# A table of moves goes out of a scheduled attention-and-MLP kernel, thresholds by segment come in, and TensorE is counted as finishing in order

## The chip, the cores and the metric

One core of one Trainium2 chip. The core has five engines with queues of their own: TensorE (PE, its weight loads shown apart as PEld), VectorE (DVE), ScalarE (ACT), GpSimd (POOL) and SyncE (SP), which issues the transfers. The metric is the device time of one launch in microseconds (us); the time before is a median of 802.64 us over three runs (802.03 to 802.87).

## What is computed

A transformer block with modulation by a condition vector, in bf16, for one sequence of 2048 rows, width 640, 32 heads of 20 columns, and an inner MLP width of 1536:

```python
mod = (silu(c) @ w_mod).reshape(1, 6, 1, 640)     # sa, ca, ga, sb, cb, gb
h = layernorm(x) * (1 + ca) + sa
q, k, v = split(h @ wqkv)                         # 32 heads of 20
o = softmax(q @ k.T * 20 ** -0.5) @ v             # 2048 x 2048 scores for each head
x = x + ga * (o @ wo)
h = layernorm(x) * (1 + cb) + sb
x = x + gb * (((h @ w_gate) * (h @ w_up)) @ w_down)
```

The scores alone are 32 x 2048 x 2048 elements, and each needs an exponential.

## The kernel before

**A scheduler in Python writes the program.** The kernel's code first makes tasks: a task is a small group of instructions of one engine with its dependencies, a modelled duration and a priority. `Sched.run` then plays the engines through in modelled time, and whatever an engine picks in that play is appended to its order (`sc.order`). `emit_program` walks over all tasks in the order of their modelled starts, gives each the semaphore waits it still needs, and writes each engine's queue. On the chip each queue runs strictly in that order; nothing is decided there.

**The work.** The 2048 query columns are cut into a chunk of 512 and six of 256. For each chunk and each of eight sets of four heads there is an item. Its work comes in units of 512 columns. A *score* group (line 2126 of the kernel before, `QT,KT`) writes units into PSUM banks. Two units at a time go to ACT, which takes the exponential of 1024 columns and writes them into a ring of 16 slots in `PP` (line 3095). The rest, about two ninths of all units, goes to DVE and POOL in quads of four units: DVE evacuates each unit as 16-bit integers into `DB` (2153), splits the quad into mantissa and exponent (2189, 2197), and a product of the mantissa part (2194 on DVE in one instruction of 2048 columns, or 2209 on POOL in four pieces of 512) gives `DSS`. A *value* group (2806, `PP,Vf` or `DSS,Vf`) multiplies both kinds with V and sums them in PSUM. At an item's end the sums are transposed and divided (2280 to 2323) into `Ocp`.

**What lies beside it.** All other TensorE work is called X by the scheduler: transposes of normalized rows (1693, 2450, 2428), projections for Q, K and V (1732, 1796, and 1536 with `wV`), modulation (1557, and 1536 with `wmb`), the output projection (`wo,Ocp`), gate and up (`h2T,stg`), and down (`wd,hprod`), the last three once for every chunk after its attention. Names ending in t belong to the next-to-last chunk, names ending in c to the last one (`h2Tc`, `hprodc`, `xckc`), whose MLP stands at the end of the program. Lines 1536 and 1532 are helpers that issue groups in 32-column tiles and in full tiles. Matmuls of `ident,Vf` (3259) add zeros and serve only to keep TensorE busy.

**How PE picks.** `pick_pe` runs whenever PE is free in the play: a score group if a pair of banks is free, else X work, value groups or filling, by thresholds that are module globals: how long PE may be held for the next score (`HOLD`), how full the exponentials' ring must be before X goes first (`XFIRST`, `XCONT`), how many value units make a group (`PVMIN`, `PVMAX`, `PVCAP`, `PVTOL`), how far an X group may delay a score (`X_LATE`, `X_HALF`), priorities of DVE's parts (`TPRIO`, `XDPRIO`) and so on. The table `STAGE` gives them values of their own for each item; `stage(it)` sets them.

**The table of moves.** After the play, `replan` edits the result: it drops 18 PE tasks, gives each task that starts after 80 us of modelled time a PSUM bank from a string of digits (`rebank`), takes tasks out of an engine's list and puts them in at other places, computes what then depends on what by bank (`rechain`), and plays the new lists through once more in their given order. The table `PLAN` holds 2034 such moves for PE, 320 for DVE, 245 for SP, 24 for POOL and 1 for ACT.

**Waits.** In `emit_program`, `kn` holds for each engine how far it knows each semaphore to have come. A wait on a task also brings what that task's engine knew when it was issued. PE has several semaphores of its own: `s_pes` for scores, `s_pep` for value groups, `s_pex` for X. What PE itself had finished on the others was not part of what it knew.

Of the kernel before, what the change touches and what calls it, by code (L numbers as in the profile page):

```python
# [37 lines left out]
T0 = 700.0  # L38
# [6 lines left out]
STEAL_END = 66197.894  # L45
# [445 lines left out]
def rebank(sc):  # L491

    k = 0
    for r in sc.G.recs:
        r["move"] = r["task"] is not None and r["task"].start >= PLAN_FROM
        if r["move"]:
            r["i"] = int(PLAN["banks"][k])
            r["put"](r["i"])
            k += 1
    assert k == len(PLAN["banks"])  # L500


def rechain(sc):

    pos = {id(t): i for i, t in enumerate(sc.order["pe"])}
    rows = {}
    for r in sc.G.recs:
        if r["task"] is None and r["i"] in (2, 5):
            continue
        rows.setdefault(r["i"], []).append((pos[id(r["task"])] if r["task"] is not None else -1, r))  # L510
    for lst in rows.values():
        lst.sort(key=lambda x: x[0])
        was = []
        for p, r in lst:
            if r["move"]:
                t = r["task"]
                old = {id(x) for x in r["rel"]}
                keep = {id(x) for x in r["base"]}
                t.deps = [x for x in t.deps if id(x) not in old or id(x) in keep]
                have = {id(x) for x in t.deps}  # L520
                t.deps = t.deps + [x for x in was if id(x) not in have]
            was = list(r["by"])


def replan(sc):
    gone = set(PLAN.get("drop", ()))
    sc.order["pe"] = [t for i, t in enumerate(sc.order["pe"]) if i not in gone]
    rebank(sc)
    for eng, moves in PLAN.items():
        if eng in ("drop", "banks"):  # L530
            continue
        old = sc.order[eng]
        gone = {a for a, _ in moves}
        new = [t for i, t in enumerate(old) if i not in gone]
        for a, b in moves:
            new.insert(b, old[a])
        sc.order[eng] = new
    rechain(sc)
    kept = {id(t) for lst in sc.order.values() for t in lst}
    span = {id(t): t.done - t.start for t in sc.all if id(t) in kept}  # L540
    left = sum(len(x) for x in sc.order.values())
    for t in sc.all:
        t.done = None
# [2823 lines left out]
```

## Time and profile before

| | |
|---|---|
| median of three runs | 802.64 us (802.03 to 802.87) |
| span of the profiled execution, first to last instruction | 800.7 us |
| DMA | 61.91 MB, mean 77 GB/s |
| exponentials on ACT (L3095) | 798 |
| evacuations of DVE's share (L2153) | 452 |
| products of a quad on DVE (L2194) | 39 |
| pieces of products on POOL (L2209) | 296 |
| matmuls | 16556 |

The profile is of one execution; the three times come from executions without it, and no time of the profiled one is given beside its span. Rows of a view by stretch read: start and end, length, then for each engine busy us and number of instructions, granted clock, share of DMA and GB/s. Rows of a timeline read: start, duration, engine, line, operation, tiles, count, and in brackets the idle time before it and who ended it. Rows of the chain read: start, duration, what. In groups by line the columns are busy us and mean ns of one, then idle time before them by releaser. A busy share of PE says that some matmul was in flight, not that PE ran at its peak.

### The profile page before, as it was taken

The page shows a single profiled execution, that of the slowest core. Times are in us where ns is not written, and L with a number is a line of the kernel's source. Part 1 is how long each engine was busy: PE and PEld are TensorE (multiplying, and loading weights), DVE is VectorE, ACT ScalarE, POOL GpSimd, SP SyncE. Part 2 cuts the span into 40 slices and gives each one's busy share as a digit, 9 for nine tenths or more (in the row PEclk, how much of TensorE's full clock was granted, in tenths as well). Part 3 has the DMA queues.
Part 4 walks back from the last instruction along what each step waited for, and adds up shares of the span by engine and source line. Part 5 has one row for each costly group of instructions (what it writes and reads, how often), then busy time and mean ns, then how long its engine had stood idle before and what let it go on. Part 6 is the DMA issues. An engine that isn't in the chain of part 4 may idle for free.

```text
span 800.7 us, 36941 instructions
## 1 busy us (share of the span) xinstructions
PE 787.5 (98%) x16556; PEld 379.1 (47%) x16556; DVE 715.3 (89%) x1308; ACT 750.8 (94%) x835; POOL 423.0 (53%) x416
## 2 busy tenths in 40 slices
PE   8999999999999999999999999999999999999998
PEld 4433523332244344444555545554556555445677
DVE  7979878888999899999989889998999999999964
ACT  6899899999999999999999999999998999999921
POOL 2327575767665655655365565545536447525610
PEclk9999999999999999999999999999999999999999
DMA  9553112112131542010223214241152224124820
GB/s 300 154 144 106 50 51 66 53 52 68 39 88 43 157 107 59 23 30 3 70 58 77 63 28 116 59 104 24 31 126 53 53 60 110 28 61 112 190 48 27
DMA packets 146093, 61.91 MB, mean 77 GB/s; under 512 B 113215, under 2 KB 145935, under 8 KB 145935
## 3 DMA queue, kind: packets, MB, share of 16 engines
q1 hardware_dynamic: 145007, 58.40, 28.7%
q8 instruction: 130, 2.13, 1.1%
q10 hardware_dynamic: 928, 1.15, 0.4%
q14 instruction: 28, 0.23, 0.1%
HBM read 50.53 MB, written 8.99 MB: 74 GB/s over the span
## 4 chain that ended last, share of the span: by engine, by line
PE 66%; ACT 22%; DVE 5%; issue 4%; DMA 1%; POOL 1%; SPq 0%; DVEq 0%; ACTq 0%
PE ps_all L2126 23%; ACT PP L3095 22%; PE ps_all L1536 20%; PE ps_all L2806 14%; PE ps_all L1796 4%; PE ps_all L1532 3%; DVE DB L2153 1%; DVE DSS L2189 1%; DVE DSS L2197 1%; POOL DSS L2209 1%; PE ps_all L1732 1%; PE ps_all L1693 1%; DMA q_rows<-KPA 1%; PE ps_all L2450 0%; DMA x<-in_A_x_dram 0%
## 5 line engine op out<-in xcount | busy, mean ns | idle before, releaser
L3095 ACT ACTIVATE PP<-ps_all 128x1024 bf16<-128x1024 f32 x798 | 734.1, 1163 | 9.7 <-PE ps_all L2806 5.0
L2209 POOL TENSOR_TENSOR DSS<-DB,DSS 128x512 bf16<-128x512 bf16 x296 | 350.3, 1208 | 273.2 <-DVE DSS L2197 229.6
L2126 PE MATMUL ps_all<-QT,KT 32*128 32x256 bf16 (+2 forms) x3648 | 322.9, 286 | 6.6 <-ACT PP L3095 1.9
L2153 DVE TENSOR_SCALAR DB<-ps_all 128x512 int16<-128x512 f32 x452 | 296.4, 680 | 34.0 <-PE ps_all L2126 32.0
L2126 PEld LDWEIGHTS ps_all<-QT,KT 32*128 32x128 bf16 x3648 | 98.0, 92 | 214.0 <-ACT PP L3095 143.0
L2806 PE MATMUL ps_all<-PP,Vf 128*32 128x256 bf16 (+3 forms) x2844 | 162.4, 288 | 0.0
L1536 PE MATMUL ps_all<-h2T,stg 128*32 128x256 bf16 (+2 forms) x2812 | 117.5, 278 | 0.2 <-DVE DB L2153 0.2
L2806 PE MATMUL ps_all<-DSS,Vf 128*32 128x256 bf16 (+3 forms) x1608 | 101.1, 288 | 0.4 <-POOL DSS L2209 0.3
L2806 PEld LDWEIGHTS ps_all<-PP,Vf 128*32 128x32 bf16 (+1 forms) x2844 | 68.1, 95 | 44.1 <-issue 37.2
L2189 DVE TENSOR_SCALAR DSS<-DB 128x2048 int16<-128x2048 int16 x113 | 86.1, 762 | 2.6
L2197 DVE TENSOR_SCALAR DSS<-DB 128x2048 int16<-128x2048 int16 x113 | 80.8, 715 | 0.2 <-PE ps_all L2806 0.2
L1536 PEld LDWEIGHTS ps_all<-h2T,stg 128*32 128x32 bf16 x2812 | 56.3, 95 | 42.5 <-issue 35.0
L1536 PE MATMUL ps_all<-wd,hprod 128*32 128x320 bf16 (+1 forms) x1396 | 59.2, 279 | 0.0
L2806 PEld LDWEIGHTS ps_all<-DSS,Vf 128*32 128x32 bf16 (+1 forms) x1608 | 44.8, 96 | 17.5 <-issue 13.5
L2194 DVE TENSOR_TENSOR DSS<-DB,DSS 128x2048 bf16<-128x2048 bf16 x39 | 48.0, 1230 | 0.4
L2291 POOL TENSOR_TENSOR OTn<-OT,invT 128x160 bf16<-128x160 f32 (+1 forms) x44 | 27.8, 650 | 19.5 <-DVE invT L2286 19.5
L1536 PEld LDWEIGHTS ps_all<-wd,hprod 128*32 128x32 bf16 x1396 | 27.1, 95 | 23.0 <-issue 17.1
L1536 PE MATMUL ps_all<-wV,hT 128*32 128x160 bf16 x1280 | 35.3, 234 | 0.0
L1796 PE MATMUL ps_all<-hT,wk 128*32 128x512 bf16 (+1 forms) x360 | 31.5, 384 | 0.0
L1796 PE MATMUL ps_all<-hT,wq 128*32 128x512 bf16 x375 | 29.8, 384 | 0.0
L1536 PEld LDWEIGHTS ps_all<-wV,hT 128*32 128x32 bf16 x1280 | 23.3, 96 | 13.6 <-issue 8.6
L1536 PE MATMUL ps_all<-wo,Ocp 128*32 128x320 bf16 (+1 forms) x660 | 29.0, 282 | 0.1
(126 smaller groups left out, 513.3 us busy)
## 6 DMA issues: line engine op xcount, KB each, us to landing
stg<-in_B_w_gate_dram SPq DMA_DIRECT2D x74, 160.0 KB
stg<-in_B_w_up_dram SPq DMA_DIRECT2D x74, 160.0 KB
KT<-k_rows SPq DMA_DIRECT2D x28, 128.0 KB
QT<-q_rows SPq DMA_DIRECT2D x48, 64.0 KB
wm<-in_w_mod_dram SPq DMA_DIRECT2D x3, 800.0 KB
x<-in_A_x_dram SPq DMA_DIRECT2D x7, 320.0 KB
k_rows<-KPA SPq DMA_DIRECT2D x16, 128.0 KB
wd<-in_B_w_down_dram SPq DMA_DIRECT2D x1, 1920.0 KB
```

What stands on the lines that cost most here:

```text
L1532: return lambda e, b: e.matmul(ps[:, b, c0:c0 + n], lhs(), rhs(), start=st, stop=sp)
L1536: return lambda e, b: e.matmul(ps[32 * x:32 * x + 32, b, c0 + o:c0 + o + w], lhs()[:, 32 * x:32 * x + 32], rhs() if w == n else rhs()[:, o ...
L1796: f = [lambda e, b_, k=k, x=x: e.matmul(ps[x:x + min(32, w - x), b_, :], wx[:, k, r0 + x:r0 + min(x + 32, w)], hT[tc][:, k, :], tile_posit ...
L2126: ems.append(lambda e, i=i, kt=kt: e.matmul(dstf()[:, i * u.n:(i + 1) * u.n], KT[32 * u.s:32 * u.s + 32, u.j, kt * 128:(kt + 1) * 128], QT ...
L2153: return e.tensor_scalar(DBl[st_["slot"]][:, x * 512:(x + 1) * 512], bank(cell["b"]), EBIAS, 0.0, op0=ALU.add, op1=ALU.max)
L2189: return e.tensor_scalar(DSl[st_["ss"][0]][:, :], DBl[st_["slot"]][:, :], 0x7F, 0x3F00, op0=ALU.bitwise_and, op1=ALU.bitwise_or)
L2194: return e.tensor_tensor(d, DBl[st_["slot"]][:, :].bitcast(BF16), d, ALU.mult)
L2197: return e.tensor_scalar(DSl[st_["ss"][1]][:, :], DBl[st_["slot"]][:, :], 0x7F80, 2, op0=ALU.bitwise_and, op1=ALU.bitwise_or)
L2209: return e.tensor_tensor(d, DBl[st_["slot"]][:, x * w:x * w + w].bitcast(BF16), d, ALU.mult)
L2291: return lambda e: e.tensor_tensor(OTn[:, g0:g0 + gn, DH * (j + x):DH * (j + x) + DH, :].rearrange("p b c r -> p b r c"), OT[:, nq_ * x:nq ...
L2806: ems.append(lambda e, i=i, kt=kt, stt=stt, stp=stp: e.matmul(ps[32 * s:32 * s + mc, binfo["bank"], c0:c0 + u.n], Vf[:, (kt * H + 4 * u.j ...
L3095: return e.activation(o, ps[:, b0:b0 + nu, :], AFT.Exp, scale=ESCALE)
```

## The change

Three parts. `PLAN`, `rebank`, `rechain` and `replan` are taken out, so that the order of the play is the order of the program. A second table of thresholds, `SEGT`, is laid over `STAGE`: `segment()` counts the exponentials that have been scheduled and sets the thresholds anew after every eight, for 76 of the hundred segments; a new threshold `XG` moves the gates of X work. And `emit_program` counts a PE task as known to PE once it is issued, on whatever semaphore: a wait for a later matmul then covers every earlier one.

```diff
-def replan(sc):
-    gone = set(PLAN.get("drop", ()))
-    sc.order["pe"] = [t for i, t in enumerate(sc.order["pe"]) if i not in gone]
-    rebank(sc)
...
             t.know[t.ctr] = t.val
+            if eng == "pe":
+                kn[t.ctr] = t.val
...
-PLAN_FROM = 80000.0
-PLAN = {
-    "drop": (1947, 1963, 2320, 2729, 3517, 3524, 4144, 4160, 4513, 4556, 4634, 4752, 4753, 5229, 5296, 5408, 5573, 5574),
...
+SEG = 8
+SEGT = {
+    1: {"PVTOL": 152.9, "XFIRST": 5},
+    2: {"HOLD": 0, "PVCAP": 10, "PVTOL": 152.9, "TPRIO": 0.538, "XFIRST": 5},
...
+    78: {"EAGER": 9, "PV_KEEP": 1},
+    79: {"PVCAP": 16, "XFIRST": 6, "X_HALF": 61.9},
...
     def stage(it):
         globals().update(base)
         globals().update(STAGE.get(it, {}))
+        globals().update(SEGT.get(seg[0], {}))
+
+    def segment():
+        while sc.progress >= SEG * (seg[0] + 1):
+            seg[0] += 1
+            stage(st_pv["item"])
...
-                    if task.gate > sc.progress or (warm and task.name[:3] == "col" and t > STEAL_END):
+                    if task.gate > sc.progress + XG or (warm and task.name[:3] == "col" and t > STEAL_END):
...
                 sc.progress = max(sc.progress, ap // 2)
+                segment()
...
     join_reads(sc)
-    replan(sc)
     nw = emit_program(nc, sc)
```

The file gets 304 lines shorter, so a line number after the tables is 312 lower in the new program up to line 2498 (2126 becomes 1814, 2806 becomes 2494, 1536 becomes 1224) and 304 lower behind that (3095 becomes 2791; 303 for the filling ones, 3259 becomes 2956).

**What it moves.** The counts of scores, exponentials on ACT, evacuations and value groups stay. Products of 2048 columns on DVE go from 39 to 53, pieces on POOL from 296 to 240. Gate and up of the middle chunks are cut more finely (matmuls of 256 columns 1880 to 1772, of 128 columns 576 to 728, of 512 columns 356 to 372), down less finely (320 columns 908 to 972, 160 columns 488 to 360). Filling goes from 40 matmuls of 512 columns to 16 of 512 and 88 of 256. ACT gets one evacuation of `hT` and one of `gsb` more. Second waits of exponentials, on `s_pep`, go from 500 to 3.

PE near the 632nd exponential, where the scores are those of the last but one chunk (`QT_78`) and the X work belongs to chunks ahead of it; before:

```order
L1536 MATMUL ps_all<-wo_109,Ocp_92 32x320 x24
L2126 MATMUL ps_all<-QT_78,KT_70 128x256 x10
L1536 MATMUL ps_all<-h2T_106,stg_110 32x256 x20
L1536 MATMUL ps_all<-h2T_106,stg_108 32x256 x20
L1536 MATMUL ps_all<-h2T_106,stg_114 32x256 x20
L1536 MATMUL ps_all<-h2T_106,stg_111 32x256 x20
L1536 MATMUL ps_all<-h2T_106,stg_114 32x256 x20
L1536 MATMUL ps_all<-h2T_106,stg_111 32x256 x8
L2126 MATMUL ps_all<-QT_78,KT_70 128x256 x10
```

and now:

```order
L1814 MATMUL ps_all<-QT_78,KT_70 128x256 x4
L2494 MATMUL ps_all<-DSS_88,Vf_83 32x256 x6
L2494 MATMUL ps_all<-DSS_88,Vf_83 21x256 x2
L1224 MATMUL ps_all<-wd_103,hprod_105 32x320 x8
L2494 MATMUL ps_all<-PP_84,Vf_83 32x256 x20
L1814 MATMUL ps_all<-QT_78,KT_70 128x256 x8
L1224 MATMUL ps_all<-wd_103,hprod_105 32x320 x28
L1224 MATMUL ps_all<-wd_103,hprod_105 32x160 x4
L1814 MATMUL ps_all<-QT_78,KT_70 128x256 x4
L2494 MATMUL ps_all<-PP_84,Vf_83 32x256 x8
```

Before, 108 gate and up matmuls stood between two score groups; now no more than 36 matmuls do, value groups included, and PE is at a down product there where it was at gate and up.

PE at the end, from the last score group (`QT_79` is the last chunk's queries) to the last block's gate and up (`h2Tc`); before:

```order
L2126 MATMUL ps_all<-QT_79,KT_70 128x128 x16
L1536 MATMUL ps_all<-h2Tt_120,stg_111 32x256 x4
L1536 MATMUL ps_all<-h2Tt_120,stg_114 32x256 x16
L2806 MATMUL ps_all<-PP_84,Vf_83 32x128 x16
L1532 MATMUL ps_all<-wo_109,Ocp_92 128x320 x12
L1536 MATMUL ps_all<-h2Tt_120,stg_114 32x256 x4
...
L2806 MATMUL ps_all<-PP_84,Vf_83 32x128 x20
L1532 MATMUL ps_all<-wo_109,Ocp_92 128x320 x6
L2428 MATMUL ps_all<-ident_49,xn2c_131 128x128 x5
L1536 MATMUL ps_all<-wd_103,hprodt_119 32x320 x100
L1532 MATMUL ps_all<-wo_109,Ocp_92 128x320 x2
```

(three groups of 20 `h2Tt` matmuls are left out, and behind the last row come 92 more `hprodt` ones), and now:

```order
L2494 MATMUL ps_all<-PP_84,Vf_83 32x128 x28
L1814 MATMUL ps_all<-QT_79,KT_70 128x128 x8
L1224 MATMUL ps_all<-wd_103,hprodt_119 32x160 x4
L1224 MATMUL ps_all<-wd_103,hprodt_119 32x320 x20
L2494 MATMUL ps_all<-PP_84,Vf_83 32x128 x28
L1220 MATMUL ps_all<-wo_109,Ocp_92 128x320 x18
L1224 MATMUL ps_all<-wd_103,hprodt_119 32x320 x16
L2494 MATMUL ps_all<-PP_84,Vf_83 32x128 x8
L1224 MATMUL ps_all<-wd_103,hprodt_119 32x320 x28
L2116 MATMUL ps_all<-ident_49,xn2c_131 128x128 x5
L1224 MATMUL ps_all<-wd_103,hprodt_119 32x320 x4
L1220 MATMUL ps_all<-wo_109,Ocp_92 128x320 x2
```

(then 64 `hprodt` and the `h2Tc` matmuls). All gate and up of the next-to-last chunk now stand ahead of the last score, and so do 48 full and 20 half down matmuls; the last score is a group of 8, not of 16.

PE near the 62nd exponential, where modulation (`wmb,SCb`) and the V projection run beside the first items; before, a part of it:

```order
L2126 MATMUL ps_all<-QT_73,KT_70 128x512 x3
L1536 MATMUL ps_all<-wmb_33_81,SCb_117 32x320 x12
L1536 MATMUL ps_all<-wmb_33_81,SCb_117 32x160 x8
L1536 MATMUL ps_all<-wmb_33_81,SCb_117 32x320 x12
L2126 MATMUL ps_all<-QT_73,KT_70 128x512 x4
L1536 MATMUL ps_all<-wmb_33_81,SCb_117 32x320 x12
L1536 MATMUL ps_all<-wV_102,hT_100 32x160 x20
L1536 MATMUL ps_all<-wmb_34_82,SCb_117 32x320 x20
L2126 MATMUL ps_all<-QT_73,KT_70 128x512 x5
L2806 MATMUL ps_all<-PP_84,Vf_83 32x512 x3
L1536 MATMUL ps_all<-wmb_34_82,SCb_117 32x320 x20
L1536 MATMUL ps_all<-wV_102,hT_100 32x160 x36
```

and now:

```order
L1814 MATMUL ps_all<-QT_73,KT_70 128x512 x2
L2956 MATMUL ps_all<-ident_49,Vf_83 32x512 x4
L1224 MATMUL ps_all<-wV_102,hT_100 32x160 x20
L1224 MATMUL ps_all<-wmb_34_82,SCb_117 32x320 x40
L2494 MATMUL ps_all<-DSS_90,Vf_83 32x512 x3
L2494 MATMUL ps_all<-DSS_90,Vf_83 21x512
L2494 MATMUL ps_all<-PP_84,Vf_83 32x512 x9
L2494 MATMUL ps_all<-DSS_89,Vf_83 32x512 x4
L2494 MATMUL ps_all<-DSS_88,Vf_83 32x512 x4
L1224 MATMUL ps_all<-wV_102,hT_100 32x160 x28
L1814 MATMUL ps_all<-QT_73,KT_70 128x512 x3
L2494 MATMUL ps_all<-PP_84,Vf_83 32x512 x8
```

Pieces of 32 to 56 X matmuls between scores have become one piece of 60, with filling ahead of it and all waiting value groups behind it.

More of the change, by code (lines that the diff above doesn't have):

```diff
@@ L488, in join_reads @@
                 r[k] = mapped(r[k])
[L491 to L522, printed above, removed]
@@ L1170 @@
+XG = 0
+SEGK = ("XG", "XFIRST", "XCONT", "PV_OPEN", "FILL_HARD")
 XHALF = 1
@@ L2940, in pick_x @@
             for task in rl:
-                if task.gate > sc.progress or (warm and task.name[:3] == "col" and t > STEAL_END):
+                if task.gate > sc.progress + XG or (warm and task.name[:3] == "col" and t > STEAL_END):
                     continue
```

132 lines of the change are left out of this document (75 added, 57 removed), and 296 rows, old and new, of the table PLAN.

## The prediction, made before the run

> **What bounds the kernel now.** I read the page's busy shares first, then the busy time by stretch, then the groups by line, the waits, and last ACT's and PE's timelines. The page:
>
> ```profile
> PE 787.5 (98%) x16556; PEld 379.1 (47%) x16556; DVE 715.3 (89%) x1308; ACT 750.8 (94%) x835; POOL 423.0 (53%) x416
> ```
>
> PE looks like the bound. It isn't for most of the span. The stretches (span's start to end; PE, PEld, DVE, ACT, POOL busy us):
>
> ```profile
> 50.00:100.00 50.00, 49.51 (x944) 20.72 (x936) 43.73 (x82) 47.11 (x52) 30.78 (x26) 1.00 0.35 96
> 100.00:600.00 500.00, 495.63 (x10219) 220.80 (x10215) 456.90 (x789) 498.66 (x544) 290.93 (x271) 1.00 0.25 64
> 600.00:625.00 25.00, 25.00 (x618) 14.44 (x611) 23.93 (x47) 21.93 (x25) 15.44 (x18) 1.00 0.41 87
> 625.00:750.00 125.00, 123.28 (x2979) 63.43 (x2978) 118.79 (x196) 125.00 (x137) 65.81 (x61) 1.00 0.32 71
> 750.00:766.20 16.20, 15.38 (x464) 10.70 (x455) 12.76 (x25) 13.94 (x15) 6.09 (x5) 1.00 0.85 189
> 766.20:800.70 34.50, 31.83 (x600) 27.37 (x597) 19.71 (x55) 3.04 (x8) 1.10 (x2) 1.00 0.07 24
> ```
>
> From 100 to 600 us ACT is busy 498.66 of 500 us and from 625 to 750 all of it; TensorE's granted clock is 1.00 throughout. What ACT does there, and who waits for it:
>
> ```profile
> L3095 ACT ACTIVATE PP<-ps_all 128x1024 bf16<-128x1024 f32 x798 | 734.1, 1163 | 9.7 <-PE ps_all L2806 5.0 <-PE ps_all L2126 4.7
> PEld ps_all L2126 <- ACT PP L3095: 143.0, 489, 0.6
> ```
>
> 798 exponentials cost 734.1 us, 0.920 each in series (their 1163 ns overlap). PE's weight loads for scores wait for ACT 489 times, 143.0 us in all: in the steady part PE's time is partly slack, in small pieces. So the span is: a head before the first exponential, the exponentials with ACT's holes, and a tail of PE work behind the last one. Only holes and tail can move, as the count of exponentials on ACT is 798 in both orders.
>
> Four places lose time. ACT's timeline at the end:
>
> ```profile
> 759.09 3.77 ACT L3095 ACTIVATE PP<-ps_all 128x1024 bf16<-128x1024 f32 x4 [0.86 <-PE ps_all L2126]
> 764.19 1.94 ACT L3095 ACTIVATE PP<-ps_all 128x1024 bf16<-128x1024 f32 x2 [1.33 <-PE ps_all L2126]
> 780.70 0.81 ACT L2436 ACTIVATE h2Tc<-ps_all,mcol 128x128 bf16<-128x128 bf16 x2 [14.57 <-PE ps_all L2428]
> ```
>
> The last exponential ends at 764.19 + 1.94 = 766.13; idle times of 0.86 + 1.33 = 2.19 us stand shortly ahead of it (hole 3). Between 766.13 and 800.7 lie 34.6 us of tail. Hole 2, at 606 us (PE, then ACT):
>
> ```profile
> 606.34 3.13 PE L1536 MATMUL ps_all<-h2T,stg 128*32 128x256 bf16 x108
> 610.90 1.94 ACT L3095 ACTIVATE PP<-ps_all 128x1024 bf16<-128x1024 f32 x2 [2.68 <-PE ps_all L2806]
> ```
>
> PE runs 108 gate/up matmuls in one piece, 3.13 us, with no score between them; ACT has two exponentials in store (1.94 us), then idles 2.68 us. With small ones ACT loses 25 - 21.93 = 3.07 us in that window. Hole 1 lies between 50 and 100 us: 50 - 47.11 = 2.89 us.
>
> **The change part by part.** Terms are against the profiled execution: span 800.7; the median 802.64 is 1.9 us above it, taken as launch and end, the same for both.
>
> (a) *Tail.* PE's part of the chain there:
>
> ```profile
> 763.82 0.35 PE ps_all L2126 x16
> 764.18 0.66 PE ps_all L1536 x20
> 765.10 1.84 PE ps_all L1532 x12
> 766.94 1.86 PE ps_all L1536 x64
> 768.80 0.47 PE ps_all L2806 x20
> 770.19 0.28 PE ps_all L2428 x5
> 770.47 3.51 PE ps_all L1536 x100
> 774.47 3.24 PE ps_all L1536 x92
> 779.60 1.00 PE ps_all L1532 x18
> 780.66 17.38 PE ps_all L1532 x252
> ```
>
> Behind the last score (763.82) PE still does 20 + 64 = 84 gate/up matmuls of the tail block, 0.66 + 1.86 = 2.52 us, and 192 down matmuls (100 + 92), 6.75 us, or 35.2 ns each. In the new order all 84 are ahead of the last score, and of the down matmuls 132 full ones and 4 of half width are left: 134 x 35.2 ns = 4.72 us. So 2.52 + 6.75 - 4.72 = **4.6 us less** PE work behind the last score. The rest there is the same in number: 36 value matmuls, 20 of the output projection, 240 gate/up and 60 down ones of the last 128-column block.
>
> That work was cover, so I ask what is late next. In DVE's timeline the last big transpose of value sums, then residual and evacuation of the first of the last two row tiles; in PE's the last projection matmuls, for the second tile:
>
> ```profile
> 762.37 0.45 DVE L2280 STREAM_TRANSPOSE OT<-ps_all 128x256 f32<-128x256 f32 x1
> 766.16 0.49 DVE L2391 TENSOR_TENSOR xckc<-ps_all,xckc 128x320 bf16<-128x320 f32 x1 [1.02 <-PE ps_all L1532]
> 770.40 1.35 DVE L2440 TENSOR_SCALAR h2Tc<-ps_all,mcol 128x128 bf16<-128x128 bf16 x5
> 773.91 0.45 PE L1532 MATMUL ps_all<-wo,Ocp 128*128 128x320 bf16 x2
> ```
>
> The first tile's chain, from 766.16 to 771.75, takes 5.6 us. In the new order PE has beside it 8 of 18 projection matmuls (1.84/12 = 0.153 us each: 1.2), 8 value matmuls (0.2), 112 down matmuls (3.9), and two projection and five transposing ones (0.6): 5.9 us. That just covers. The projection itself now stands directly behind a group of value matmuls, with 56 value, 24 down and 8 score matmuls (1.3 + 0.8 + 0.2 = 2.3 us by these rows) between the value sums it needs and itself, where before it started 765.10 - 762.37 = 2.7 us behind their transpose. I put 1.5 us of new PE idle time, between 0 and 4.6 (all of the gain given back). The second tile's chain, from the last projection matmuls to its last evacuation, is covered by 64 down matmuls and 120 gate/up ones: 2.3 + 120 x 1.00/18 = 8.9 us, against the 7.6 from 773.91 to 781.51 (ACT's row of h2Tc above). **Tail: -3.1**, ends -4.6 and 0. The work pulled ahead of the last score lies beside ACT, in the 143.0 us of slack.
>
> (b) *Hole 2.* The run of 108 is gone; near that point no more than 36 matmuls now stand between two scores, 36 x 35.2 ns = 1.3 us, under the 1.94 that ACT holds in store. **-3.0**, ends -3.07 and 0.
>
> (c) *Hole 1.* Here the new order has one clump ahead of a value wait: 4 filling matmuls, 20 V and 40 modulation ones, 4 + 9 for value sums. With the rows below (3.4/40, 3.6/84, 35.3/1280 us each; value matmuls of 512 columns like the filling ones) it is 0.34 + 0.55 + 1.71 + 1.1 = 3.7 us, less 1.94 in store: 1.8 us of ACT idle in place of 2.89. **-1.0**, ends -2.89 and +2.
>
> ```profile
> L3259 PE MATMUL ps_all<-ident,Vf 128*32 128x512 bf16 x40 | 3.4, 384 | 0.0
> L1536 PE MATMUL ps_all<-wmb,SCb 128*32 128x320 bf16 (+1 forms) x84 | 3.6, 294 | 0.1
> L1536 PE MATMUL ps_all<-wV,hT 128*32 128x160 bf16 x1280 | 35.3, 234 | 0.0
> L2194 DVE TENSOR_TENSOR DSS<-DB,DSS 128x2048 bf16<-128x2048 bf16 x39 | 48.0, 1230 | 0.4
> L1699 ACT ACTIVATE hT<-ps_all,mcol 128x512 bf16<-128x512 bf16 x5 | 3.8, 778 | 4.8 <-PE ps_all L1693 4.8
> ```
>
> (d) *Hole 3.* The last scores now stand every 8 matmuls, with 0.3 to 1.1 us of other work between. I take **-1.5**; ends -2.19 (closed) and +4.6, if all that (a) pulls ahead lands in front of these scores.
>
> (e) *ACT.* One more hT evacuation, 778 ns: **+0.7**, ends 0 (ACT idle there) and +0.8. A gsb cast more, behind the last exponential: 0.
>
> (f) *DVE and POOL.* 14 more products of 2048 columns on DVE, 14 x 1.230 = 17.2 us, in place of 56 pieces on POOL. DVE's rows above leave it 43.1 us between 100 and 600 and 6.2 between 625 and 750, 49.3 in all. Where it was fullest (118.79 of 125) ACT still ran 125.00. I take **0**; ends 0 and +17.2.
>
> (g) *Filling and narrower pieces.* Fill goes from 40 x 512 columns to 16 x 512 and 88 x 256: 40 to 60 full ones, 20 x 3.4/40 = 1.7 us more PE time, in PE's gaps beside ACT: **0**, ends 0 and +1.7. The split forms carry as many columns as before.
>
> (h) *Waits.* 500 of 798 exponentials had a second wait, on the value matmuls that had read their buffer; 3 keep one. The value matmuls stand ahead of the score on PE, so the score's own wait ends later. The row of L3095 shows 5.0 us of idle time by that releaser, of it 2.68 in hole 2, already counted. **0**, ends -2.3 and 0.
>
> POOL's pieces show what the two engines do to each other:
>
> ```profile
> L2209 POOL TENSOR_TENSOR DSS<-DB,DSS x296: 1145/1157/2199, 50.3 to 760.0; 128x512 bf16<-128x512 bf16 x148
> ```
>
> The median piece, 1157, is nearly the fastest, so they seldom disturb each other. [...]
>
> Sum: -3.1 - 3.0 - 1.0 - 1.5 + 0.7 = -7.9; 802.64 - 7.9 = **794.8**.
>
> **The rivals.**
> *All holes close and the tail is covered*: -4.6 - 3.07 - 2.89 - 2.19 = -12.8, 789.9. For it: each hole has one run of PE work as its cause. Against: the clump in (c).
> *The tail turns from PE work to its chains*: (a) gives nothing and (d) nothing: 802.64 - 3.0 - 1.0 + 0.7 = 799.3. For it: 5.9 us of cover over a chain of 5.6.
> *DVE sets the pace, and the kernel is slower*: it evacuates the scores of its own share, and PE's banks stay held until it has. It decides once more than 6.2 us of new products fall into a stretch as full as 625 to 750. With half of the 17.2 on the path, and the four gains lost as scores come late, 802.64 + 8.6 = 811; with the gains kept it would be 803.3. Against: 49.3 us free, and POOL waits for DVE, not DVE for POOL.
> *New holes elsewhere*: the whole order is made anew, so waits that the scheduler does not foresee fall in new places. Two or three more like hole 2 (3.07 each): 800.9 to 804.0.
> *The thresholds change nothing*: excluded, PE's order has 2885 rows in place of 2772.
>
> **How the numbers follow.** Forecast (792 to 798) 0.40; chains in the tail 0.18; all closed 0.14; new holes 0.15 (of it 0.05 still faster); DVE 0.13 (0.01 of it no change). A difference of 0.2% (1.6 us) is about what a measurement of this kernel tells from none. Faster: 0.40 + 0.18 + 0.14 + 0.05 = 0.77; same 0.11; slower 0.12. The range runs from 790 to 803: below it half of "all closed" (0.07), above it nearly all of DVE's case (0.12).
>
> **What would show it.** Right: the new page's ACT idle before L2791 (the exponential's new line) well under 9.7; no run of gate/up matmuls over 2 us near 606; last exponential near 761 and some 31 to 32 us from there to the end. Wrong in (a): idle PE in the tail ahead of the projection or of the last block's gate/up matmuls. Wrong in (f): DVE over 98% in several stretches while ACT loses time there with scores as releaser. Wrong altogether: ACT's holes as large, in other places.

## The result and the profile after

798.22 us, the median of four executions (797.22 to 799.35), beside 802.43 for the kernel before on the same chip: a ratio of 0.9945, 95% interval 0.9931 to 0.9959. Run again twelve times beside the first experiments it took 797.74 us, ratio 0.9955 (0.9939 to 0.9971). The kernel is faster by 4.2 to 4.5 us; 7.8 were forecast, and the range (790 to 803) holds the time.

The page of the kernel after, busy time by engine:

```profile
PE 785.2 (98%) x16628; PEld 381.1 (48%) x16628; DVE 715.7 (90%) x1320; ACT 752.1 (94%) x837; POOL 340.7 (43%) x360
```

The stretches of before, now of after (span's start to end; PE, PEld, DVE, ACT, POOL busy us; clock; DMA):

```profile
50.00:100.00 50.00, 48.59 (x897) 19.72 (x889) 43.51 (x83) 43.02 (x48) 20.76 (x20) 0.97 0.29 76
100.00:600.00 500.00, 496.68 (x10427) 225.26 (x10423) 460.97 (x802) 498.62 (x544) 233.82 (x231) 1.00 0.26 66
600.00:625.00 25.00, 24.72 (x558) 12.84 (x552) 23.35 (x46) 24.58 (x28) 10.22 (x13) 1.00 0.09 24
625.00:750.00 125.00, 124.05 (x3054) 67.19 (x3052) 116.97 (x200) 124.77 (x137) 51.79 (x53) 1.00 0.35 80
750.00:766.20 16.20, 15.95 (x496) 10.47 (x491) 13.94 (x25) 16.20 (x18) 6.25 (x6) 1.00 0.50 108
766.20:797.60 31.40, 28.62 (x475) 24.27 (x462) 18.07 (x52) 3.62 (x10) 1.10 (x2) 1.00 0.07 23
```

Three of the four places came out near the forecast. ACT's idle time at 600 to 625 us fell from 3.07 to 0.42 us, that of the last stretch before the tail from 2.2 to nothing, and the tail got shorter. The fourth went the other way: between 50 and 100 us ACT was idle for 2.89 us and now is for 6.98, with a granted clock of 0.97 in that row. ACT's timeline there, at hole 2's place and at the end (start, duration, operation, count; in brackets the idle time before it and who ended it):

```profile
59.73 1.02 ACT L2791 ACTIVATE PP<-ps_all 128x1024 bf16<-128x1024 f32 x1 [1.38 <-PE ps_all L1814]
62.09 1.94 ACT L2791 ACTIVATE PP<-ps_all 128x1024 bf16<-128x1024 f32 x2 [1.34 <-PE ps_all L1814]
64.69 2.87 ACT L2791 ACTIVATE PP<-ps_all 128x1024 bf16<-128x1024 f32 x3 [0.67 <-PE ps_all L1814]
68.05 16.61 ACT L2791 ACTIVATE PP<-ps_all 128x1024 bf16<-128x1024 f32 x18 [0.48 <-PE ps_all L1814]
87.76 4.69 ACT L2791 ACTIVATE PP<-ps_all 128x1024 bf16<-128x1024 f32 x5 [3.11 <-PE ps_all L2494]
...
612.44 13.19 ACT L2791 ACTIVATE PP<-ps_all 128x1024 bf16<-128x1024 f32 x14 [0.27 <-PE ps_all L1814]
...
749.62 16.78 ACT L2791 ACTIVATE PP<-ps_all 128x1024 bf16<-128x1024 f32 x18
```

The last exponential ends at 749.62 + 16.78 = 766.40, so the tail is 797.6 - 766.4 = 31.2 us in place of 34.6. Hole 1 is now two things. At 84.65 us stands the clump that the prediction named, 3.11 us where it said 1.8. Ahead of it lie four pieces, 3.87 us together, which it didn't name. They begin here (the chain of waits between 52 and 61 us: start, duration, what):

```profile
52.83 0.42 SPq L1783
...
53.29 5.13 DMA KT<-k_rows
...
58.55 0.37 PE ps_all L1814
```

The same score in TensorE's timeline, with the idle time before it:

```profile
58.55 0.37 PE L1814 MATMUL ps_all<-QT,KT 32*128 32x512 bf16 x1 [1.30 <-DMA KT<-k_rows]
```

A `KT` load is issued at 53.29, behind seven `wo` loads (L1783) on SP's queue, takes 5.13 us to land, and a score waits for it; TensorE is idle for 1.30 us. Two microseconds later its clock falls (the stretches from 60 to 65 us, columns as above; the clock is the first number behind POOL's):

```profile
60.00:61.00 1.00, 1.00 (x19) 0.37 (x18) 0.25 (x1) 0.75 (x1) 0.00 (x0) 0.88 0.13 33
61.00:62.00 1.00, 1.00 (x12) 0.14 (x6) 0.87 (x2) 0.00 (x0) 0.00 (x0) 0.50 0.58 115
62.00:63.00 1.00, 1.00 (x24) 0.58 (x22) 0.45 (x2) 0.91 (x1) 0.49 (x1) 0.50 0.29 101
63.00:64.00 1.00, 1.00 (x12) 0.17 (x7) 1.00 (x3) 1.00 (x2) 0.67 (x1) 0.50 0.23 80
64.00:65.00 1.00, 1.00 (x14) 0.22 (x10) 0.94 (x2) 0.33 (x2) 0.00 (x0) 0.91 0.00 0
```

0.24 us of the first row, three whole ones and 0.18 of the last: 3.4 us at half clock. Not every execution has this, as the first run below shows.

### The profile page after: what moved, and what is told of

Its sections match the earlier page's. It is cut to its first block, busy times and chain, and to the rows that moved or that the text cites. A ratio compares the mean times of both kernels' runs of the same rounds, so it can differ in the third digit from the quotient of the medians.

```text
span 797.6 us, 36503 instructions
## 1 busy us (share of the span) xinstructions
PE 785.2 (98%) x16628; PEld 381.1 (48%) x16628; DVE 715.7 (90%) x1320; ACT 752.1 (94%) x837; POOL 340.7 (43%) x360
## 4 chain that ended last, share of the span: by engine, by line
ACT 49%; PE 43%; DVE 6%; DMA 1%; SPq 1%; issue 0%; DVEq 0%
ACT PP L2791 48%; PE ps_all L1814 14%; PE ps_all L1224 12%; PE ps_all L2494 9%; PE ps_all L1220 3%; PE ps_all L1484 2%; DVE DB L1841 2%; DMA KT<-k_rows 1%; PE ps_all L1420 1%; DVE DSS L1882 1%; DVE DSS L1877 1%; DVE DSS L1885 1%; SPq L1783 1%; DMA x<-in_A_x_dram 1%; PE ps_all L2138 0%; PE ps_all L1245 0%
## 5 line engine op out<-in xcount | busy, mean ns | idle before, releaser
L1897 POOL TENSOR_TENSOR DSS<-DB,DSS 128x512 bf16<-128x512 bf16 x240 | 273.0, 1157 | 341.9 <-DVE DSS L1885 276.9
L1841 DVE TENSOR_SCALAR DB<-ps_all 128x512 int16<-128x512 f32 x452 | 301.7, 683 | 37.9 <-PE ps_all L1814 35.4
L1814 PE MATMUL ps_all<-QT,KT 32*128 32x256 bf16 (+2 forms) x3648 | 316.8, 287 | 6.3 <-ACT PP L2791 3.3
L1814 PEld LDWEIGHTS ps_all<-QT,KT 32*128 32x128 bf16 x3648 | 93.1, 92 | 205.3 <-ACT PP L2791 177.2
L1224 PE MATMUL ps_all<-h2T,stg 128*32 128x256 bf16 (+2 forms) x2872 | 124.5, 275 | 0.1
L2494 PE MATMUL ps_all<-DSS,Vf 128*32 128x256 bf16 (+2 forms) x1608 | 91.7, 289 | 0.0
L2494 PEld LDWEIGHTS ps_all<-PP,Vf 128*32 128x32 bf16 (+1 forms) x2844 | 56.9, 95 | 66.6 <-issue 60.7
L1877 DVE TENSOR_SCALAR DSS<-DB 128x2048 int16<-128x2048 int16 x113 | 79.4, 703 | 0.4
L1885 DVE TENSOR_SCALAR DSS<-DB 128x2048 int16<-128x2048 int16 x113 | 77.5, 686 | 2.1 <-PE ps_all L2494 2.1
L1224 PEld LDWEIGHTS ps_all<-h2T,stg 128*32 128x32 bf16 x2872 | 62.6, 96 | 32.5 <-issue 27.9
L1882 DVE TENSOR_TENSOR DSS<-DB,DSS 128x2048 bf16<-128x2048 bf16 x53 | 65.6, 1241 | 0.2
```

Source lines behind the costliest of these rows:

```text
L1224: return lambda e, b: e.matmul(ps[32 * x:32 * x + 32, b, c0 + o:c0 + o + w], lhs()[:, 32 * x:32 * x + 32], rhs() if w == n else rhs()[:, o ...
L1814: ems.append(lambda e, i=i, kt=kt: e.matmul(dstf()[:, i * u.n:(i + 1) * u.n], KT[32 * u.s:32 * u.s + 32, u.j, kt * 128:(kt + 1) * 128], QT ...
L1841: return e.tensor_scalar(DBl[st_["slot"]][:, x * 512:(x + 1) * 512], bank(cell["b"]), EBIAS, 0.0, op0=ALU.add, op1=ALU.max)
L1877: return e.tensor_scalar(DSl[st_["ss"][0]][:, :], DBl[st_["slot"]][:, :], 0x7F, 0x3F00, op0=ALU.bitwise_and, op1=ALU.bitwise_or)
L1882: return e.tensor_tensor(d, DBl[st_["slot"]][:, :].bitcast(BF16), d, ALU.mult)
L1885: return e.tensor_scalar(DSl[st_["ss"][1]][:, :], DBl[st_["slot"]][:, :], 0x7F80, 2, op0=ALU.bitwise_and, op1=ALU.bitwise_or)
```

## The experiments

The edits of the order stand behind `join_reads`. `put` takes tasks of one engine's order (by their number) and puts them behind another task of it; `merge` merges the five orders again by their dependencies, so that waits are counted anew.

**The changed kernel again**, no edit.

> The changed kernel as it is, run again beside the three that follow, so that they stand against it on one chip. Its time should be 797.2 to 799.4 us and its ratio to the kernel before 0.993 to 0.996. If the fall of TensorE's granted clock near 61 us follows from the order, it is there in this profile too, with 7 us of ACT idle time between 50 and 100 us; if it comes and goes from one execution to the next, this profile may show 1.00 there, and about 1 to 2 us less idle time.

797.74 us. Of its twelve executions eight ran at a mean clock of 1.000, with spans of 795.1 to 796.3 us, three at 0.998 (797.2 to 799.0) and one at 0.989 (803.2). The profiled one had 1.000, and the stretch from 50 to 100 us reads

```profile
50.00:100.00 50.00, 49.37 (x926) 20.16 (x918) 45.01 (x86) 45.03 (x49) 22.89 (x22) 1.00 0.29 76
58.78 1.02 ACT L2791 ACTIVATE PP<-ps_all 128x1024 bf16<-128x1024 f32 x1 [0.59 <-PE ps_all L1814]
60.63 4.69 ACT L2791 ACTIVATE PP<-ps_all 128x1024 bf16<-128x1024 f32 x5 [0.82 <-PE ps_all L1814]
85.43 7.44 ACT L2791 ACTIVATE PP<-ps_all 128x1024 bf16<-128x1024 f32 x8 [3.10 <-PE ps_all L2494]
```

(the stretch, then ACT's timeline). Same order, 2.0 us less idle time on ACT. Of it 0.8 us is the KT load, for which TensorE waits 0.51 us here and waited 1.30 there; the other 1.2 us go with the clock. The fall of the clock comes and goes. Executions with it take some 2 us longer; how much of that is a late KT load is known for the profiled one only. Against this span of 795.2 the change is worth 5.5 us. Below, the time between 50 and 100 us is compared with this profile.

**KT ahead of eight wo loads.**

```diff
     join_reads(sc)
+    put(sc, "sp", [([50, 51, 52, 53, 54, 55, 56, 59], 89)])
+    merge(sc)
```

> The changed kernel with eight wo loads (56 to 58 KB each as a group of 0.42 us issues) moved on SP's queue from 48 to 57 us to behind 74 us, so that the KT load that TensorE waits for at 58.55 us (1.30 us idle) is issued about 1 us earlier and has the queues to itself. Theory A (the wo loads in front of it on SP and beside it in the queues delay KT): the 1.30 us of TensorE idle time goes, and with it most of ACT's 3.9 us of idle time between 58 and 68 us and the low clock behind it: 2 to 4 us faster than the changed kernel, 794 to 796 us. Rival (KT waits for the landing of its own k_rows write, or the clock alone makes the loss): the idle time stays within 0.3 us and the time within 1 us of the changed kernel.

(The 56 to 58 KB are a misreading: one of these loads moves 5 to 25 KB.) 797.16 us (796.3 to 797.8), ratio 0.9933 (0.992 to 0.9946). The KT load is issued at 51.93 us, not at 52.80, and TensorE no longer waits for it; ACT's row for 50 to 100 us is 45.81 in place of 45.03, and all five executions had a clock of 1.000:

```profile
50.00:100.00 50.00, 49.87 (x936) 20.32 (x928) 45.62 (x87) 45.81 (x50) 23.51 (x22) 1.00 0.29 76
```

So the place of the KT load behind the `wo` loads is the cause of 0.8 us there. It is less than theory A said: of its 3.9 us some 1.2 went with the clock and 0.8 with a KT load that landed later still than in the profile above. The whole time is 0.6 us below the changed kernel's, and the two intervals overlap, so a gain in time isn't shown. In this execution ACT also has 0.95 us of new idle time at 228.7 us; two of the runs below have the same edit and not this idle time, so it isn't shown to follow from the edit. As to the clock: in the fifteen executions of the three runs that have this edit and all the filling it never fell, and in the thirty-eight of the five that have the early order without it, it fell in eight. That points to the KT load, without being enough to show it.

**Value matmuls ahead of the modulation ones**, at the clump.

```diff
+    put(sc, "dve", [([172], 169)])
+    put(sc, "pe", [(range(659, 667), 644), ([683], 651), ([694], 675)])
+    merge(sc)
```

> The changed kernel with eight value matmuls moved ahead of the 40 modulation ones near the 62nd exponential, the next two scores moved forward accordingly, and on VectorE the evacuation that frees their PSUM bank moved ahead of two casts. Theory A (the 3.11 us of ACT idle time at 84.65 us is the run of TensorE work in front of the value matmuls that release the exponential's buffer): the hole shrinks from 3.11 to about 1.9 us, what is left is the wait for the bank; 1 to 1.3 us faster than the changed kernel. Rival (the hole is set by VectorE or GpSimd, which the order on TensorE does not touch): the idle time between 84 and 92 us stays at 3.1 us in sum, only split, and the time is the same within 0.3 us.

798.71 us (797.9 to 801.0), ratio 0.9957 (0.9945 to 0.9969). ACT's timeline:

```profile
84.44 2.86 ACT L2821 ACTIVATE PP<-ps_all 128x1024 bf16<-128x1024 f32 x3 [2.10 <-PE ps_all L2524]
87.65 1.02 ACT L2821 ACTIVATE PP<-ps_all 128x1024 bf16<-128x1024 f32 x1 [0.36 <-PE ps_all L1844]
90.25 3.78 ACT L2821 ACTIVATE PP<-ps_all 128x1024 bf16<-128x1024 f32 x4 [1.57 <-PE ps_all L1844]
```

The hole shrinks by 1.0 us, near what theory A said, and 0.36 + 1.57 us stand behind it. TensorE is busy for 5.45 of the 5.60 us from 84.4 to 90: what was put behind the value matmuls now stands ahead of the next scores. Theory A didn't have that; its rival had that the hole would only be split, but not why. In the 2.10 us that are left TensorE itself waits 0.43 us for VectorE's evacuation of `Vf`.

**Both edits.**

> Both edits in one kernel. If the two losses are independent, their gains add: 3 to 5 us faster than the changed kernel, 793 to 795 us, which is what was forecast for the change with its first hole closed. If the second hole only takes what the first leaves (ACT catches up on scores already waiting), the gain is that of the larger edit alone.

798.3 us, ratio 0.9945 (0.9933 to 0.9957): no sum, and nothing gained over the changed kernel.

**Work taken out of the stretch**: the first edit, and 40 modulation matmuls, whose result nobody needs before 260 us, moved to 150 and 182 us in two groups (their banks' holders before and after are swapped in the dependencies).

```diff
+    put(sc, "sp", [([50, 51, 52, 53, 54, 55, 56, 59], 89)])
...
+    put(sc, "pe", [(range(659, 667), 644), ([683], 675), ([694], 682), (range(650, 655), 1190), (range(645, 650), 1445)])
+    put(sc, "dve", [([172], 169), ([175], 286), ([173], 339)])
```

> The changed kernel with the later wo loads of the second run, and with the 40 modulation matmuls near the 62nd exponential (and the two casts behind them) moved out of the first 100 us, in two groups of 20, to 150 and 182 us, where ACT has no holes; nothing needs their result before 260 us. The eight value matmuls then stand right behind the 20 V ones. Theory L (between 50 and 100 us TensorE's whole work is the bound, so only work that leaves the stretch shortens it): the 3.10 us of ACT idle time shrinks by about 40 x 35 ns = 1.4 us and does not come back behind it; 1 to 2 us faster than the run with the wo loads alone, 795 to 796.5 us, and no new hole at 150 or 182 us. Rival (the wait for the bank or for GpSimd's pieces sets the hole): within 0.5 us of the run with the wo loads alone.

798.1 us, ratio 0.9946 (0.9933 to 0.9959). ACT's timeline, and TensorE's at the first of the new places:

```profile
83.90 3.77 ACT L2821 ACTIVATE PP<-ps_all 128x1024 bf16<-128x1024 f32 x4 [2.09 <-PE ps_all L2524]
88.29 7.65 ACT L2821 ACTIVATE PP<-ps_all 128x1024 bf16<-128x1024 f32 x8 [0.61 <-PE ps_all L1844]
153.55 4.87 ACT L2821 ACTIVATE PP<-ps_all 128x1024 bf16<-128x1024 f32 x5 [0.62 <-PE ps_all L1844]
186.92 3.77 ACT L2821 ACTIVATE PP<-ps_all 128x1024 bf16<-128x1024 f32 x4 [0.70 <-PE ps_all L1844]
...
151.47 0.86 PE L1254 MATMUL ps_all<-wmb,SCb 128*32 128x320 bf16 x20
```

The hole falls from 3.10 to 2.09 + 0.61, by 0.4 us where theory L had about 1.4. And a group of 20, which holds TensorE for 0.69 us until the next group starts, makes 0.62 us of idle time on ACT at 150 us, where there was none, and 0.70 at 186, where there was 0.38. Theory L was right on the stretch in tendency, wrong in size, and wrong on the rest of the kernel: at these two places there was no slack to put the work into. By its time the rival holds.

**No thresholds from the 704th exponential on.**

```diff
+SEGT = {k: v for k, v in SEGT.items() if k < 88}
```

> The changed kernel without the thresholds from the 704th exponential on; everything before them is the same. Behind the last score stand 40 gate/up, 58 down, 28 value and 32 filling matmuls more than in the changed kernel. Theory A (the tail is TensorE work alone, and the late thresholds closed the tail and the hole before it): the tail grows from 31.16 us by 40 x 35 ns + 58 x 35 ns and some 0.5 us, about 4 us, and the ACT idle time before the last exponentials is 0 to 2 us: 4 to 6 us slower than the changed kernel. Rival (the tail is a chain through VectorE and ACT that this work lies beside): at most 1.5 us slower.

804.03 us, ratio 1.0019 (1.0002 to 1.0037), some 6 us above the changed kernel. ACT's last exponentials:

```profile
761.21 7.58 ACT L2794 ACTIVATE PP<-ps_all 128x1024 bf16<-128x1024 f32 x8 [1.66 <-PE ps_all L2497]
```

They end at 768.79, and the span is 804.3: the tail is 35.5 us, 4.3 more than 31.2 where about 4 were expected, and hole 3 is back with 1.66 us. Theory A holds: the tail is as long as TensorE's work behind the last score.

**No thresholds at all.**

```diff
+SEGT = {}
```

> The changed kernel with no thresholds by eight exponentials at all: neither moves nor own thresholds. If the thresholds do what the moves did before, this is slower than both kernels: behind the last score there are 120 gate/up and 192 down matmuls in place of 136 down ones, about 6 us more in the tail, and holes come back elsewhere: 805 to 815 us. Rival (the scheduler alone orders the work as well, thresholds and moves are worth little): 797 to 801 us.

810.0 us, ratio 1.0088 (1.0075 to 1.0101). The table of thresholds is worth some 12 us against the scheduler alone; a hole of 5.51 us at 611 us and a tail of 37.2 us, in place of 0.42 and 31.2, are over 11 us of that. The hole at 611 us stands beside a run of 152 gate and up matmuls, 4.33 us long.

**Hole 2 split in the kernel before.** Its table of moves stays; then

```diff
     replan(sc)
+    put(sc, "dve", [([1003], 999)])
+    put(sc, "pe", [([4676], 4658), (range(4685, 4689), 4665), ([4677], 4668), (range(4700, 4704), 4675), ([4704], 4680), ([4710], 4694)])
+    merge(sc)
```

> The kernel before, with one edit near 606 us: on TensorE three scores and two groups of value matmuls are moved into the run of 108 gate/up matmuls, and on VectorE one evacuation of scores is moved ahead of three other instructions; the table of moves stays. Theory A (term (b): that run is what ACT's 2.68 us of idle time is made of): the hole shrinks to 1 us or less and the kernel is 1.6 to 2.6 us faster than before. Rival (ACT then waits for the next scores, as all of TensorE's work there has to be done anyway): the idle time between 600 and 625 us stays near 3 us, split in several pieces, and the time within 0.5 us of before.

804.56 us, ratio 1.0021 (1.0013 to 1.003): slower than before. ACT's timeline:

```profile
609.92 1.94 ACT L3125 ACTIVATE PP<-ps_all 128x1024 bf16<-128x1024 f32 x2 [0.92 <-PE ps_all L2836]
612.58 1.02 ACT L3125 ACTIVATE PP<-ps_all 128x1024 bf16<-128x1024 f32 x1 [0.71 <-PE ps_all L2156]
613.89 1.02 ACT L3125 ACTIVATE PP<-ps_all 128x1024 bf16<-128x1024 f32 x1 [0.29 <-PE ps_all L2156]
616.40 3.78 ACT L3125 ACTIVATE PP<-ps_all 128x1024 bf16<-128x1024 f32 x4 [1.49 <-PE ps_all L2156]
```

In place of one hole of 2.68 us there are four, 3.41 together. The rival was right: splitting the run of 108 doesn't close the hole.

**The same with 68 gate and up matmuls left out.**

```diff
+    for i in [*range(4691, 4699), 4712, 4713, *range(4719, 4723), 4725, 4726, 4727]:
+        sc.order["pe"][i].emits = []
```

> The edit near 606 us in the kernel before once more, and with it 68 of the 328 gate/up, projection and down matmuls between 600 and 625 us left out of the computation (gate and up of two hidden tiles of one block are incomplete). Theory L (the stretch has more TensorE work than fits beside ACT, the run of 108 is only where it shows): ACT's idle time between 600 and 625 us falls from 4.2 us in the run with the edit alone by about 68 x 32 ns = 2.2 us, to 2 us or less, and the time by 1.5 to 2.5 us against that run. Rival (the new order of scores or of VectorE makes the pieces of idle time): it stays within 0.7 us of 4.2.

803.86 us, ratio 1.0016 (1.0004 to 1.0028). Six of its twelve executions fell to a clock of 0.994 to 0.996; the six at 1.000 took 802.3 to 803.0 us, some 2 us less than the run with the split alone. The stretch, of that run and then of this one:

```profile
600.00:625.00 25.00, 24.73 (x579) 13.48 (x568) 22.18 (x45) 20.84 (x23) 13.76 (x17) 1.00 0.40 86
```

```profile
600.00:625.00 25.00, 23.39 (x527) 12.46 (x526) 22.67 (x46) 21.30 (x23) 14.95 (x18) 1.00 0.40 80
```

ACT's idle time falls only from 4.16 to 3.70 us, and TensorE is now idle for 1.6 us itself (0.56 for a gate evacuation on VectorE, 0.68 for ACT). So it isn't the amount of TensorE work alone either. My order of scores and evacuations there makes waits of its own; the rest of the 2 us lies in other stretches (1.0 us of ACT's idle time ahead of 100 us, between these two profiles), where nothing was changed. What exactly made hole 2 stays open. One rival is not tested: that the change put less other work into this stretch. Counted from the starts of the matmuls, TensorE spent 11.2 us between 600 and 625 us on work other than scores and values in the kernel before (204 gate and up matmuls among it), spends 10.2 us in the changed kernel (48), and 12.6 us in the run without thresholds (224); ACT's idle time there is 3.07, 0.42 and 5.51 us. The length of the longest run goes the same way, and no run separates the two.

**Second waits back**, in the changed kernel.

```diff
-            if eng == "pe":
-                kn[t.ctr] = t.val
```

> The changed kernel with TensorE no longer counted as finishing in order (two lines of the emitter taken out), so that some 500 exponentials wait again for the value matmuls that read their buffer as well as for their score; the order of work is the same. Forecast, term (h): the value matmuls stand ahead of the score on TensorE, so the second wait ends first: the same time within 0.5 us. Rival (a second wait costs ACT its own time, or ends late at some places): 0.5 to 5 us slower than the changed kernel.

797.33 us, ratio 0.9933 (0.9921 to 0.9945), 0.4 us from the changed kernel: no difference.

**All products on VectorE.**

```diff
-X_POOL, X_PIECES, POOL_NS = 1, 4, 1.95
+X_POOL, X_PIECES, POOL_NS = 0, 4, 1.95
```

> The changed kernel with GpSimd's share of the products taken over by VectorE: no pieces on GpSimd, about 60 more products of 1.24 us on VectorE, 74 us more by the rows. Third rival of the prediction (VectorE sets the pace once its idle time is used up): 715.7 + 74 = 790 us of VectorE work leaves it nothing, and the kernel is 10 to 30 us slower, with VectorE over 98 % busy in most stretches. [...]

819.99 us, ratio 1.0218 (1.0205 to 1.0231). The page's first line, VectorE's two masks of a quad (busy us, mean ns of one) and a stretch:

```profile
PE 800.7 (98%) x16856; PEld 394.1 (48%) x16856; DVE 765.1 (94%) x1380; ACT 753.7 (92%) x837; POOL 72.1 (9%) x120
...
L1885 DVE TENSOR_SCALAR DSS<-DB 128x2048 int16<-128x2048 int16 x113 | 76.4, 676 | 1.9 <-PE ps_all L2494 1.9
L1877 DVE TENSOR_SCALAR DSS<-DB 128x2048 int16<-128x2048 int16 x113 | 76.6, 678 | 0.3
```

```profile
100.00:600.00 500.00, 491.87 (x10229) 225.68 (x10227) 482.86 (x822) 489.63 (x533) 45.08 (x61) 1.00 0.24 62
```

ACT loses 10.4 us between 100 and 600 us with VectorE busy for 482.9 of 500, 96.6%: that fits the third rival. But the edit changes what the scheduler plays, so the order of all engines is made anew, and about half of the 22 us that it loses lies in the tail: the last exponential ends at 775.9 us, and from there to the end it takes 42.3 us in place of 31.2, with TensorE busy for 48.6 of the last 52. So this run doesn't price the third rival by itself. VectorE's busy time grew by 49.4 us where the rows of its products made 74.

**No filling behind 50 us**, with the KT edit.

```diff
+    gone = {id(t) for t in sc.order["pe"] if t.name == "zfill" and t.start > 50000}
+    sc.order["pe"] = [t for t in sc.order["pe"] if id(t) not in gone]
```

> The changed kernel with the later wo loads of the second run and without the 104 filling matmuls behind 50 us (16 of 512 columns between 60 and 85 us, 88 of 256 columns at 249 to 260, 519 to 521 and 667 to 670 us); they add zeros, nothing of the result is left out. Theory L (where ACT has holes, TensorE's work is the bound, and elsewhere ACT is): the 16 early ones free about 16 x 64 ns = 1.0 us, of it 0.27 us lies beside a wait for a bank: 0.5 to 0.8 us less ACT idle time between 50 and 100 us than in the run with the wo loads alone, the 88 others give nothing, and the time is 0.5 to 1 us lower, 796.2 to 796.7 us. Rival (the filling keeps TensorE's clock up, or lies in waits): the granted clock falls below 1.00 somewhere and the time rises by 1 us or more, or the time stays within 0.3 us.

802.58 us, 795.9 to 807.6, ratio 0.9994 (0.9966 to 1.0021). One of twelve executions kept the full clock; it took 795.94 us, the shortest time of any in this study. The others had mean clocks of 0.981 to 0.996. In the profiled one (0.991; columns as above):

```profile
250.00:252.00 2.00, 1.39 (x31) 0.50 (x26) 2.00 (x5) 2.00 (x3) 0.46 (x1) 1.00 0.48 63
252.00:254.00 2.00, 1.41 (x26) 0.37 (x18) 2.00 (x5) 2.00 (x4) 0.00 (x0) 1.00 1.01 349
254.00:256.00 2.00, 1.71 (x19) 0.65 (x21) 1.74 (x4) 2.00 (x3) 0.00 (x0) 0.51 1.07 397
...
266.00:268.00 2.00, 2.00 (x28) 0.48 (x26) 0.70 (x2) 1.25 (x2) 0.31 (x1) 0.57 0.00 0
268.00:270.00 2.00, 2.00 (x45) 0.83 (x46) 1.89 (x4) 1.93 (x3) 0.00 (x0) 1.00 0.00 0
```

TensorE is idle for 1.2 us of four, in pieces of 0.2 to 0.5 us in front of scores, and then runs at half clock for 13.7 us. The rival was right on the clock: without the filling matmuls it falls in eleven of twelve executions, and in the profiled one it falls where ACT had been busy without a pause. What the filling costs is small. Between 50 and 100 us ACT is busy for 45.42 us without it and for 45.81 with it, so theory L's gain isn't there, and the one execution at full clock is 0.4 to 1.8 us shorter than the five of the KT edit.

No kernel here is faster than the changed one by more than these runs can tell; the KT edit comes nearest.

## Why the prediction was right, and where it was not

The time came out in the range. Of the signs that the prediction named, the tail of 31.2 us is there and so is the end of the long run near 606 us. The first one is weak: ACT's idle time before the exponentials was to be well under 9.7 us, and the last exponential was to end near 761 us. The row of the exponentials, in the first profile and in the one at full clock:

```profile
L2791 ACT ACTIVATE PP<-ps_all 128x1024 bf16<-128x1024 f32 x798 | 734.2, 1147 | 9.3 <-PE ps_all L1814 5.4
L2791 ACT ACTIVATE PP<-ps_all 128x1024 bf16<-128x1024 f32 x798 | 734.0, 1152 | 7.2 <-PE ps_all L2494 3.4
```

At full clock the holes give 2.5 us together and the last exponential ends at 764.0; the larger part of the gain is the tail. (802.64 - 7.9 makes 794.7; the prediction puts down 794.8, a slip of no weight.)

Against the profile at full clock (span 795.2), by the prediction's terms:

| term | forecast | measured |
|---|---|---|
| (a) tail | -3.1 | -3.4 |
| (b) hole 2, 600 to 625 us | -3.0 | -2.7 |
| (c) hole 1, 50 to 100 us | -1.0 | **+2.1** |
| (d) hole 3 | -1.5 | -2.2 |
| (e) one evacuation more on ACT | +0.7 | +0.8 (what is left) |
| other small holes | 0 | -0.1 |
| sum | -7.9 | -5.5 |

**(c) was mis-sized**, by 3.1 us, which is more than the whole difference between the two sums; the other terms give 0.7 us back. Two steps of it failed.

"0.34 + 0.55 + 1.71 + 1.1 = 3.7 us, less 1.94 in store: 1.8 us of ACT idle": the clump is there, but there was nothing in store. ACT ended the 62nd exponential of the trace at 84.65, before the clump began at 85.03; the 63rd and 64th had their scores, and waited for the very value matmuls behind the clump to free their slots of the ring. A store of two counts only if those two wait for nothing in the clump. That makes 3.1 for 1.8.

Nothing was said of SP, although the change takes 245 moves away from its queue. That put seven `wo` loads, which nobody needs before 87 us, ahead of a KT load that a score waits for (in the kernel before all `wo` loads are issued between 104 and 204 us): 0.8 us by the KT edit, of about 1.8 that lie there. In the first profile the clock falls behind it (0.97 in the row from 50 to 100 us), and executions with a mean clock of 0.998 take some 2 us more (spans of 797.2 to 799.0 us beside 795.1 to 796.3 at 1.000); the median of 797.74 lies 0.7 us above the profiled execution of 796.99.

**(a) and (d) were right by their reason, (a) with some luck in its size.** The profile shows no wait of TensorE's in the new tail, so none of the 1.5 us of new idle time that I put in came. Counted from the start of the last score, as the 4.6 us were, the tail went from 36.9 to 32.7 us, so the work that went was worth 4.2. Counted from the end of the last exponential it is 3.4, because the last score is now a group of 8 with one exponential behind it, not of 16 with two. That -3.4 lies near -3.1 is the sum of these misses. The run without the late thresholds brings both terms back with the matmuls counted for it.

**(b) was right in size, and its reason isn't shown.** It said that the run of 108 is gone and that no more than 36 matmuls stand between two scores. Splitting the run in the kernel before didn't help, and in the changed kernel less other work stands in the stretch as well.

**(f) was right:** VectorE's busy time hardly moved, 715.3 to 715.7, though 17.2 us of products were added. Part of it is that its masks got shorter, by 10.0 us in all, with 56 pieces fewer on GpSimd (rows of before, then of after); the rest is not traced:

```profile
L2189 DVE TENSOR_SCALAR DSS<-DB 128x2048 int16<-128x2048 int16 x113 | 86.1, 762 | 2.6
L2197 DVE TENSOR_SCALAR DSS<-DB 128x2048 int16<-128x2048 int16 x113 | 80.8, 715 | 0.2 <-PE ps_all L2806 0.2
```

```profile
L1877 DVE TENSOR_SCALAR DSS<-DB 128x2048 int16<-128x2048 int16 x113 | 79.4, 703 | 0.4
L1885 DVE TENSOR_SCALAR DSS<-DB 128x2048 int16<-128x2048 int16 x113 | 77.5, 686 | 2.1 <-PE ps_all L2494 2.1
```

The means go from 762 and 715 ns with 296 pieces over 703 and 686 with 240 to 678 and 676 with none. Why the masks get shorter isn't shown. The products' mean goes from 1230 ns before to 1241 after, and to 1212 with no pieces.

**(h) was right:** 0.4 us with the second waits back.

**One step was wrong without a term of its own:** that TensorE has 143.0 us of slack beside ACT, read from its weight loads' waits for ACT. The rows of the matmuls themselves say otherwise (waits of PE for ACT, before and after):

```profile
PE ps_all L2126 <- ACT PP L3095: 1.9, 8, 0.4
```

```profile
PE ps_all L1814 <- ACT PP L2791: 3.3, 13, 0.5
```

Of the weight loads' 143.0 us before, 139.8 lie beside a matmul in flight, by the starts and ends in the trace. From the starts of all matmuls in the trace I worked out how long TensorE spends from a score group's first matmul to the next other one. A group that waited for nothing took 0.32 to 0.34 us, whether of 2 or of 8 matmuls:

| | before | after, full clock |
|---|---|---|
| score groups | 776 | 783 |
| their time, us | 271.5 | 264.4 |
| at 0.32 us each | 248 | 251 |
| all other matmuls, us | 524.8 | 526.4 |

So the real slack was at most some 23 us and is now at most 14. The groups take 7.1 us less (some 9 us less of waiting, and 2 more for seven groups more), and with 1.6 us more of other work that is the 5.5 us of the change. Both engines are nearly full from 100 to 750 us: by the rows of the first profile TensorE is busy for 645.5 of the 650 us and ACT for 648.0. That would explain why the lumps of the experiments on hole 1 had nowhere to go; no run tests it by itself.

## What to carry to other kernels

A wait of TensorE's weight loads isn't slack by itself: here they waited 143.0 us for ACT, the score matmuls 1.9 us. Measure it between the matmuls. Where TensorE and ACT are both full, work moved out of one hole can open others, as it did in three of the edits here (0.36 and 1.57 us behind the clump, 0.62 us at 150 us, four holes of 3.41 us together for one of 2.68). Work counts as "in store" over a clump only if it waits for nothing inside the clump: here the hole was 3.11 us where 1.8 were forecast. When an order is made anew, read the queue that issues the transfers with the same care as the engines.

## What the runs showed of the hardware that was not expected

TensorE's granted clock fell to half behind little idle time: one piece of 1.30 us in the profiled execution of the changed kernel, pieces of 0.2 to 0.5 us that add up to 1.2 us of four in that of the run without filling. It stayed at half for 3.4 us in the one and for 13.7 us, four times as long, in the other. The same program has a fall in some executions only: the mean clock was below 1.000 in four of twelve of the changed kernel run again, and in eleven of twelve without the filling. In the profile of the changed kernel that kept its clock, TensorE waited 0.51 us for the KT load where it waited 1.30 us in the other. What makes the clock fall, and what ends it, no run shows.

In the traces of before and after, a score group took TensorE at least 0.317 us for 2 matmuls of 512 columns and 0.325 us for 8 of 128.
